# Linear-memory attention and two expert layers on one core: the second softmax computed for both halves of the heads at once, and a diagonal by ScalarE

## The chip, the core and the metric

The kernel runs on one core of a Trainium2 chip. Its engines are TensorE (PE in the profile; its weight loads are PEld), VectorE (DVE), ScalarE (ACT), GpSimd (POOL) and SyncE (SP, which here only issues DMAs). The metric is the time of one execution on the device in microseconds (us); lower is better.

## What is computed

Three layers, each fed by the one before. The attention has 4 batches of 8 heads, 576 positions, head size 64, and 32 memory slots: a first softmax over the positions turns `phi` into weights that gather keys and values into the memories, a second softmax over the 32 slots weights the values' memories. A gated layer follows, then a layer of 8 experts, each token going to one of them.

```python
def _attn_ref(q, k, v, phi):                      # 4 x 8 x 576 x 64; phi 4 x 8 x 576 x 32
    a = np.exp(phi - np.max(phi, axis=2, keepdims=True))
    a = a / (np.sum(a, axis=2, keepdims=True) + 1e-09)
    k_m = np.einsum('bhsm,bhsd->bhmd', a, k)
    v_m = np.einsum('bhsm,bhsd->bhmd', a, v)
    scores = 1.0 / np.sqrt(q.shape[-1]) * np.matmul(q, k_m.transpose(0, 1, 3, 2))
    attn = np.exp(scores - np.max(scores, axis=-1, keepdims=True))
    attn = attn / (np.sum(attn, axis=-1, keepdims=True) + 1e-09)
    return np.matmul(attn, v_m)

def _moe_ref(x, w_gate, w_val, w_out):            # x 2304 x 512, inner size 1536
    g = x @ w_gate
    return g * (1.0 / (1.0 + np.exp(-g))) * (x @ w_val) @ w_out
...
def _moe2_ref(x, w_gate, w1, w2, capacity):       # 8 experts, inner size 1024
    expert_idx = np.argmax(x @ w_gate, axis=1)
...
        out[i] = gate_w[i] * (np.maximum(x[i] @ w1[e], 0.0) @ w2[e])
```

All large matmuls are done in three passes over a high and a low part of each operand (`PASSES`), so every operand is split first: the high part by ScalarE (L115), the low part by VectorE or GpSimd (L119).

## The kernel before

The program is written as Python generators that emit instructions; a scheduler then decides the order of the instructions on each engine, and at run time each engine works through its own queue in that order. So the order in which a change's operations are emitted, and how long the scheduler takes them to be, can move other instructions too.

`attention(b)` (L254) emits one batch. The 8 heads are two halves `Q` of four, and the 576 positions two blocks `n` of `NB` = 288 columns.

- `peak(Q)` (L273) takes the maxima of `phi`: `mx` by VectorE over the positions in a partition, a transpose on TensorE into `pmx`, `top` by VectorE. To spread the 128 maxima over all partitions it makes the diagonal matrix `dg` = identity times `top` (L282, VectorE, 128x128) and multiplies it by ones on TensorE (L283). For b >= 1 ScalarE copies the result to `mg` (L285).
- `powers(Q)` (L287) subtracts (GpSimd for b >= 1, VectorE for b = 0) and takes the exponential, `ex`. `memories(Q)` (L320) multiplies `ex` by the raw keys and values `kvraw`; `normal(Q)` scales by the reciprocal sums into `kvs`; `turned(Q)` transposes into `tk` (keys) and `tv` (values).
- `queries(Q, n)` (L392) transposes q into `qt`; `products(Q, n)` (L407) multiplies: `psc`, 128 partitions (4 heads x 32 slots) x 288 columns.
- `softmax_1(Q, n)` and `softmax_2(Q, n)` (L422, L435) are the second softmax for one half and one block. VectorE turns blocks of 32x32 so that the slots lie along the free axis (`sA`, L429), takes the maxima of the 9 groups (L431), subtracts them (L432); ScalarE takes the exponential (L433); VectorE sums (L441), adds 1e-9 and inverts the 9 sums (L442, L443), multiplies (L444) and turns back into `af` (L445). For the first two batches `af` is split at once into `at`.

Eight instructions on VectorE and one on ScalarE, 16 times. `af`/`at` is the moving operand of the gated layer: `moe_in` (L632) multiplies it by `mh` (the gate's and the value's weights with the values' memories multiplied in, `mem_in` L591) into `pg` and `pv` (L644), and makes `gh` of them (`sg`: ScalarE L652, VectorE L653 and L654). `moe_out` (L658) multiplies `gh` by `wo`.

`moe_pair` (L1049) does two batches together, the inner size in 3 groups of 4 tiles of 128 columns. Batch 0's attention stands at the start, alone. Batch 1's is emitted in steps between the gate steps of batch 0 (the first half of group 0), batches 2 and 3 between the steps of the groups that follow, one step (one `yield`) per gate step. Between them all stand the weights' loads and splits: `split64` (L128) rebuilds a weight tile from its raw words by ScalarE (`mag`, L136), three VectorE instructions (L137, L139, L140) and a split, ScalarE and GpSimd.

Buffers that matter: `ph` and `kvraw` of batches 1 to 3 share two buffers (`traw`), so the next batch's `ph` waits until the memories of the batch before are multiplied; `sA`, `gh`, `qt`, `af` and others share nine (`t46`); `psc`, `pm`, `pq`, `pt`, `pmx` share four PSUM banks (`aux`).

Of the kernel before, what the change touches and what calls it, by code (L numbers as in the profile page):

```python
# [8 lines left out]
F32 = mybir.dt.float32  # L9
# [3 lines left out]
AF = mybir.ActivationFunctionType  # L13
# [8 lines left out]
def attention_moe_moe_kernel(  # L22
# [16 lines left out]
    nc = tc.nc  # L39
# [214 lines left out]
    def attention(b):  # L254
# [18 lines left out]
        def peak(Q):  # L273
# [7 lines left out]
            dg = sb.tile([128, 128], F32, tag="dg", name="dg", bufs=2)  # L281
            nc.vector.tensor_scalar(dg, ident, top, None, ALU.mult)  # L282
            nc.tensor.matmul(pm[:, 128:256], ones, dg, start=True, stop=True)  # L283
# [123 lines left out]
        def products(Q, n):  # L407
            psc = pscs[Q, n] = aux("psc")
            for hp in range(2):
                nc.tensor.matmul(psc[:, :NB], tks[Q][:, hp], qts[Q, n][:, hp], start=(hp == 0), stop=(hp == 1))  # L410

        def scores(Q, n):
            products(Q, n)
            softmax(Q, n)

        def softmax(Q, n):
            softmax_1(Q, n)
            softmax_2(Q, n)

        sAs = {}  # L420

        def softmax_1(Q, n):  # L422
            ns = slice(n * NB, (n + 1) * NB)
            psc = pscs[Q, n]
            NK = NB // MM
            sA = sAs[Q, n] = t46([128, 2, NK, MM], "sA")
            s1, s2 = sA[:, 0], sA[:, 1]
            f1 = s1.rearrange("p k m -> p (k m)")
            nc.vector.transpose(f1, psc[:, :NB])  # L429
            m1 = sb.tile([128, NK], F32, tag="m1", name="m1", bufs=2)  # L430
            nc.vector.tensor_reduce(m1, s1, AX.X, ALU.max)  # L431
            nc.vector.tensor_sub(s2, s1, m1.unsqueeze(2).to_broadcast([128, NK, MM]))  # L432
            nc.scalar.activation(s1, s2, AF.Exp, scale=float(D) ** -0.5)  # L433

        def softmax_2(Q, n):  # L435
            ns = slice(n * NB, (n + 1) * NB)
            NK = NB // MM
            s1, s2 = sAs[Q, n][:, 0], sAs[Q, n][:, 1]
            f2 = s2.rearrange("p k m -> p (k m)")
            m2 = sb.tile([128, NK], F32, tag="m1", name="m2", bufs=2)  # L440
            nc.vector.tensor_reduce(m2, s1, AX.X, ALU.add)  # L441
            nc.vector.tensor_scalar(m2, m2, 1e-9, None, ALU.add)  # L442
            nc.vector.reciprocal(m2, m2)  # L443
            nc.vector.tensor_mul(s2, s1, m2.unsqueeze(2).to_broadcast([128, NK, MM]))  # L444
            nc.vector.transpose(af[:, Q, ns], f2)  # L445
            if first:
                split(af[:, Q, ns], at[:, Q, 0, ns], at[:, Q, 1, ns], pool=True)

# [4 lines left out]
        if b == 0:  # L453
# [20 lines left out]
            products(0, 0)  # L474
            softmax_1(0, 0)
            memories(1, (1,))
            advance(p1, 1)
            softmax_2(0, 0)
            normal(1)
            queries(0, 1)  # L480
            queries(1, 1)
            advance(p1, ALL)
            turned(1)
            products(1, 0)
            softmax_1(1, 0)
            preps[0] = w
            yield
            products(0, 1)
            softmax_2(1, 0)
            softmax_1(0, 1)  # L490
            products(1, 1)
            softmax_2(0, 1)
            softmax_1(1, 1)
            softmax_2(1, 1)
            return
# [17 lines left out]
        yield  # L513
        scores(0, 0)
        turned(1)
        yield
        queries(1, 0)
        load_q(1)
        yield
        scores(1, 0)  # L520
        queries(0, 1)
        yield
        scores(0, 1)
        queries(1, 1)
        yield
        scores(1, 1)
        yield
# [707 lines left out]
```

## Time and profile before

| | |
|---|---|
| median of 3 runs | 779.68 us (779.32 to 781.97) |
| the profiled execution | 775.05 us, of which span 773.20 |
| mean granted TensorE clock | 0.95 of full |
| busy: TensorE | 698.3 us (90%), 5232 matmuls |
| busy: VectorE | 516.6 us (67%), 1156 instructions |
| busy: ScalarE | 364.8 us (47%), 763 instructions |
| busy: GpSimd | 258.3 us (33%), 286 instructions |

The shares are means over stages that differ much. In forty slices of 19.3 us the page gives the busy share in tenths (9 is 90% or more):

```profile
PE   5658878996889999979999999998999999999992
DVE  4998798989895775876076387466458556555640
ACT  2454445665642663546264075345256454444540
POOL 2465184437540360445043035131252212101101
PEclk9768887999999999999999999999999999999996
```

The attention lies in the first 13 slices. PEclk is the clock that TensorE was granted.

### The profile page before, as it was taken

To read this page: it belongs to the slowest core of one execution; us is meant where nothing else is said; L and a number is where in the kernel's file an instruction comes from. 1 tells how busy PE (TensorE), PEld (TensorE's weight loads), DVE (VectorE), ACT (ScalarE), POOL (GpSimd) and SP (SyncE) were. 2 spreads that over 40 slices of the span, in tenths; PEclk is the share of its full clock that TensorE was granted. 3 is DMA by queue.
4 is the path that set the end of the run, shared out by engine and by line. 5 is a ranking of instruction groups with operands and counts; after the bars stand their busy time and mean duration, and the time that the engine had idled before them with its cause. 6 is when DMAs were issued, how large, how long until landed. Compare 5 with 4: busy or idle time off the path is not lost. (4 is left out here: it accounts for less than half of the span.)

```text
span 773.2 us, 14235 instructions
## 1 busy us (share of the span) xinstructions
PE 698.3 (90%) x5232; PEld 663.5 (86%) x5232; DVE 516.6 (67%) x1156; ACT 364.8 (47%) x763; POOL 258.3 (33%) x286
## 2 busy tenths in 40 slices
PE   5658878996889999979999999998999999999992
PEld 4547657995889999979999998988989999999981
DVE  4998798989895775876076387466458556555640
ACT  2454445665642663546264075345256454444540
POOL 2465184437540360445043035131252212101101
PEclk9768887999999999999999999999999999999996
DMA  9977959997730621797998043153298746555520
GB/s 236 260 177 248 244 195 306 306 339 293 224 152 23 250 77 32 171 122 159 317 245 268 16 149 103 50 137 82 40 320 268 245 150 221 194 160 185 170 87 27
DMA packets 90089, 140.12 MB, mean 181 GB/s; under 512 B 28639, under 2 KB 66143, under 8 KB 84640
## 3 DMA queue, kind: packets, MB, share of 16 engines
q1 hardware_dynamic: 82560, 104.25, 46.4%
q0 software_dynamic: 7456, 34.92, 15.7%
q8 instruction: 43, 0.70, 0.5%
q14 instruction: 30, 0.25, 0.1%
HBM read 103.61 MB, written 35.79 MB: 180 GB/s over the span
## 5 line engine op out<-in xcount | busy, mean ns | idle before, releaser
L665 PE MATMUL py<-gh,wo 128*128 128x288 f32 x1152 | 165.3, 299 | 2.1 <-DVE sg L653 2.1
L665 PEld LDWEIGHTS py<-gh,wo 128*128 128x128 f32 x1152 | 156.1, 188 | 4.1 <-DVE sg L653 2.6
L644 PE MATMUL pg<-at,mh 128*128 128x288 f32 x576 | 105.2, 310 | 21.2 <-DVE sg L653 16.6
L119 POOL TENSOR_TENSOR gh<-sg,gh 128x288 fp32r<-128x288 f32 x96 | 82.7, 870 | 94.4 <-ACT gh L115 91.3
L912 PE MATMUL p<-xt,w1h 128*128 128x288 f32 x768 | 111.0, 300 | 1.0 <-DVE hh L117 1.0
L938 PE MATMUL p<-hh,w2h 128*128 128x288 f32 x768 | 108.0, 298 | 1.3 <-ACT w2h L115 1.0
L644 PEld LDWEIGHTS pg<-at,mh 128*128 128x128 f32 x576 | 85.9, 195 | 26.8 <-DVE sg L653 19.2
L644 PE MATMUL pv<-at,mh 128*128 128x288 f32 x576 | 102.7, 305 | 3.4 <-DVE sg L654 2.7
L912 PEld LDWEIGHTS p<-xt,w1h 128*128 128x128 f32 x768 | 104.2, 190 | 1.5 <-DVE hh L117 1.2
L938 PEld LDWEIGHTS p<-hh,w2h 128*128 128x128 f32 x768 | 103.2, 188 | 2.0 <-ACT w2h L115 1.3
L644 PEld LDWEIGHTS pv<-at,mh 128*128 128x128 f32 x576 | 87.2, 196 | 5.5 <-DVE sg L654 3.8
L119 DVE TENSOR_TENSOR w2h<-w2r,w2h 128x1024 fp32r<-128x1024 f32 x36 | 42.4, 1220 | 48.1 <-ACT w2h L115 48.0
L653 DVE SCALAR_TENSOR_TENSOR sg<-sg,pg 128x288 f32<-128x288 f32 x96 | 42.5, 449 | 46.2 <-ACT sg L652 45.2
L119 DVE TENSOR_TENSOR mh<-pm,mh 64x512 fp32r<-64x512 f32 (+1 forms) x92 | 62.9, 685 | 9.3 <-ACT mh L115 7.3
L652 ACT ACTIVATE sg<-pg 128x288 f32<-128x288 f32 x96 | 38.5, 409 | 64.6 <-PE pg L644 39.7
L123 POOL DMA_INDIRECT out_dram<-ot,idx x24 | 23.7, 986 | 116.3 <-DVE ot L954 113.5
L115 ACT ACTIVATE mh<-pm 64x512 fp32r<-64x512 f32 (+1 forms) x92 | 54.1, 590 | 12.1 <-PE pm L616 4.6
L675 DVE TENSOR_TENSOR yp<-py,yp 128x288 f32<-128x288 f32 x64 | 28.9, 454 | 36.8 <-PE py L665 36.2
L115 ACT ACTIVATE gh<-sg 128x288 fp32r<-128x288 f32 x96 | 41.9, 442 | 24.3 <-DVE sg L654 16.5
L119 DVE TENSOR_TENSOR w1h<-w1r,w1h 128x1024 fp32r<-128x1024 f32 x36 | 43.0, 1221 | 12.6 <-ACT w1h L115 12.5
L123 POOL DMA_INDIRECT perm<-tokid,addr x24 | 23.9, 996 | 78.8 <-DVE addr L744 46.3
L115 ACT ACTIVATE hh<-p 128x288 fp32r<-128x288 f32 x64 | 25.7, 408 | 43.1 <-PE p L912 41.3
(206 smaller groups left out, 1067.0 us busy)
## 6 DMA issues: line engine op xcount, KB each, us to landing
w1r<-in_moe_w_dram SPq DMA_DIRECT2D x36, 512.0 KB, 5.0
w2r<-in_moe_w_dram SPq DMA_DIRECT2D x36, 512.0 KB, 4.6
wgv<-wsc POOLq DMA_DIRECT2D x14, 1024.0 KB, 9.6
wsc<-wgv SPq DMA_DIRECT2D x12, 1024.0 KB, 6.8
wo<-osc POOLq DMA_DIRECT2D x10, 1024.0 KB, 10.2
wr<-in_moe_w_gate_dram SPq DMA_DIRECT2D x12, 512.0 KB, 5.2
wr<-in_moe_w_val_dram SPq DMA_DIRECT2D x12, 512.0 KB, 6.1
wor<-in_moe_w_out_dram SPq DMA_DIRECT2D x12, 512.0 KB, 4.3
```

What stands on the lines that cost most here:

```text
L115: nc.scalar.activation(hi, src, AF.Relu if relu else AF.Copy)
L119: (nc.gpsimd if pool else nc.vector).tensor_sub(lo, src, hi.bitcast(F32))
L123: ins = nc.gpsimd.indirect_dma_start(*args, **kwargs)
L644: nc.tensor.matmul(pg[gv][:, :NB], mh[:, a, Q, gv * 128 : gv * 128 + 128], at[:, Q, c, ns], start=(Q == 0 and n3 == 0), stop=(Q == 1 and n ...
L652: nc.scalar.activation(sg, pg[0][:, :NB], AF.Tanh, scale=0.5 / 256)
L653: nc.vector.scalar_tensor_tensor(sg, sg, 1.0, pg[0][:, :NB], ALU.add, ALU.mult)
L665: nc.tensor.matmul(py[:, :NB], ws[i // 2][:, i % 2, a, d * 128 : d * 128 + 128], gh[:, c, ns], start=(i == 0 and n3 == 0), stop=(i == len( ...
L675: nc.vector.tensor_add(yp[:, d], py[:, :NB], yp[:, d])
L912: nc.tensor.matmul(p1[:, :NB], st["w1"][d][:, a, f * 128 : f * 128 + 128], st["xt"][d][:, c], start=(d == 0 and n3 == 0), stop=(d == NDT - ...
L938: nc.tensor.matmul(p2[:, :NB], w2h[f // 2][:, f % 2, a, d * 128 : d * 128 + 128], hh[f][:, c], start=(f == 0 and n3 == 0), stop=(f == NF2 ...
```

## The change

The second softmax takes both halves of the heads in one tile `sA` of [128, 2, 2, 9, 32], where one half had [128, 2, 9, 32]. The transposes stay one per half (the products lie in two PSUM banks); the maxima, the subtraction, the exponential, the sums, the add, the reciprocal and the multiply become one instruction each for 576 elements (18 groups). So a block's softmax now starts when both halves' products are there. The steps are arranged anew: a batch has nine `yield`s in place of ten, with `queries` of both halves ahead of `scores(n)`, which emits both products and the softmax. Apart from that `dg` is made by ScalarE, as a copy with the scale `top`, in place of VectorE. The work of TensorE, GpSimd and the DMAs is the same; their order changes where the scheduler moves them.

```diff
@@ -279,7 +279,7 @@
             top = sb.tile([128, 1], F32, tag="top", name="top", bufs=2)
             nc.vector.tensor_reduce(top, pm[:, :128], AX.X, ALU.max)
             dg = sb.tile([128, 128], F32, tag="dg", name="dg", bufs=2)
-            nc.vector.tensor_scalar(dg, ident, top, None, ALU.mult)
+            nc.scalar.activation(dg, ident, AF.Copy, scale=top)
             nc.tensor.matmul(pm[:, 128:256], ones, dg, start=True, stop=True)
             if b >= 1:
                 nc.scalar.copy(mg[:, hs].rearrange("p h m -> p (h m)"), pm[:, 128:256])
@@ -409,42 +409,38 @@
             for hp in range(2):
                 nc.tensor.matmul(psc[:, :NB], tks[Q][:, hp], qts[Q, n][:, hp], start=(hp == 0), stop=(hp == 1))
 
-        def scores(Q, n):
-            products(Q, n)
-            softmax(Q, n)
-
-        def softmax(Q, n):
-            softmax_1(Q, n)
-            softmax_2(Q, n)
+        def scores(n):
+            products(0, n)
+            products(1, n)
+            softmax_1(n)
+            softmax_2(n)
 
         sAs = {}
-
-        def softmax_1(Q, n):
+        NK = NB // MM
+
+        def softmax_1(n):
+            sA = sAs[n] = t46([128, 2, 2, NK, MM], "sA")
+            s1, s2 = (sA[:, i].rearrange("p q k m -> p (q k) m") for i in range(2))
+            for Q in range(2):
+                nc.vector.transpose(sA[:, 0, Q].rearrange("p k m -> p (k m)"), pscs[Q, n][:, :NB])
+            m1 = sb.tile([128, 2 * NK], F32, tag="m1", name="m1", bufs=2)
+            nc.vector.tensor_reduce(m1, s1, AX.X, ALU.max)
+            nc.vector.tensor_sub(s2, s1, m1.unsqueeze(2).to_broadcast([128, 2 * NK, MM]))
+            nc.scalar.activation(s1, s2, AF.Exp, scale=float(D) ** -0.5)
+
+        def softmax_2(n):
             ns = slice(n * NB, (n + 1) * NB)
-            psc = pscs[Q, n]
-            NK = NB // MM
-            sA = sAs[Q, n] = t46([128, 2, NK, MM], "sA")
-            s1, s2 = sA[:, 0], sA[:, 1]
-            f1 = s1.rearrange("p k m -> p (k m)")
-            nc.vector.transpose(f1, psc[:, :NB])
-            m1 = sb.tile([128, NK], F32, tag="m1", name="m1", bufs=2)
-            nc.vector.tensor_reduce(m1, s1, AX.X, ALU.max)
-            nc.vector.tensor_sub(s2, s1, m1.unsqueeze(2).to_broadcast([128, NK, MM]))
-            nc.scalar.activation(s1, s2, AF.Exp, scale=float(D) ** -0.5)
-
-        def softmax_2(Q, n):
-            ns = slice(n * NB, (n + 1) * NB)
-            NK = NB // MM
-            s1, s2 = sAs[Q, n][:, 0], sAs[Q, n][:, 1]
-            f2 = s2.rearrange("p k m -> p (k m)")
-            m2 = sb.tile([128, NK], F32, tag="m1", name="m2", bufs=2)
+            sA = sAs[n]
+            s1, s2 = (sA[:, i].rearrange("p q k m -> p (q k) m") for i in range(2))
+            m2 = sb.tile([128, 2 * NK], F32, tag="m1", name="m2", bufs=2)
             nc.vector.tensor_reduce(m2, s1, AX.X, ALU.add)
             nc.vector.tensor_scalar(m2, m2, 1e-9, None, ALU.add)
             nc.vector.reciprocal(m2, m2)
-            nc.vector.tensor_mul(s2, s1, m2.unsqueeze(2).to_broadcast([128, NK, MM]))
-            nc.vector.transpose(af[:, Q, ns], f2)
-            if first:
-                split(af[:, Q, ns], at[:, Q, 0, ns], at[:, Q, 1, ns], pool=True)
+            nc.vector.tensor_mul(s2, s1, m2.unsqueeze(2).to_broadcast([128, 2 * NK, MM]))
+            for Q in range(2):
+                nc.vector.transpose(af[:, Q, ns], sA[:, 1, Q].rearrange("p k m -> p (k m)"))
+                if first:
+                    split(af[:, Q, ns], at[:, Q, 0, ns], at[:, Q, 1, ns], pool=True)
 
         if b == 0:
             tvs["alone"] = ttv()
@@ -472,26 +468,19 @@
             p0, p1 = prep_split(w, wrs, 0), prep_split(w, wrs, 1)
             advance(p0, ALL)
             products(0, 0)
-            softmax_1(0, 0)
             memories(1, (1,))
             advance(p1, 1)
-            softmax_2(0, 0)
             normal(1)
             queries(0, 1)
             queries(1, 1)
-            advance(p1, ALL)
             turned(1)
             products(1, 0)
-            softmax_1(1, 0)
+            softmax_1(0)
+            advance(p1, ALL)
             preps[0] = w
+            softmax_2(0)
             yield
-            products(0, 1)
-            softmax_2(1, 0)
-            softmax_1(0, 1)
-            products(1, 1)
-            softmax_2(0, 1)
-            softmax_1(1, 1)
-            softmax_2(1, 1)
+            scores(1)
             return
         peak(0)
         peak(1)
@@ -511,19 +500,16 @@
         normal(1)
         queries(0, 0)
         yield
-        scores(0, 0)
         turned(1)
-        yield
         queries(1, 0)
+        yield
         load_q(1)
-        yield
-        scores(1, 0)
+        scores(0)
+        yield
         queries(0, 1)
-        yield
-        scores(0, 1)
         queries(1, 1)
         yield
-        scores(1, 1)
+        scores(1)
         yield
 
     def attention_done(b):
```

The scheduler's order, up to batch 3, changes on every engine; behind that it is the same. Two places show how.

VectorE, around the first block's softmax of batch 1 (`sA` and `m` are its tiles, `mx` the maxima of batch 2's `phi`, `mh` the gate weights of batch 0's last tile, `tv` batch 1's values). Before:

```order
L429 STREAM_TRANSPOSE sA<-psc 128x288
L119 TENSOR_TENSOR mh<-pm,mh 128x512
L431 TENSOR_REDUCE m_742<-sA 128x9
L119 TENSOR_TENSOR tv<-pt,tv 128x64
L432 TENSOR_TENSOR sA<-sA,m_742 128x288
L119 TENSOR_TENSOR tv<-pt,tv 128x64
L275 TENSOR_REDUCE mx<-ph 128x128
L441 TENSOR_REDUCE m_746<-sA 128x9
L275 TENSOR_REDUCE mx<-ph 128x128
L442 TENSOR_SCALAR m_746<-m_746 128x9
```

With the change (its own line numbers: L425 to L441 are the softmax, L639 and L640 are `sg`):

```order
L275 TENSOR_REDUCE mx<-ph 128x128 x2
L640 SCALAR_TENSOR_TENSOR sg<-sg,pv 128x288
L119 TENSOR_TENSOR tv<-pt,tv 128x64
L140 SCALAR_TENSOR_TENSOR mag<-mag,wor 128x512
L119 TENSOR_TENSOR mh<-pm,mh 128x512
L639 SCALAR_TENSOR_TENSOR sg<-sg,pg 128x288
L119 TENSOR_TENSOR tv<-pt,tv 128x64
L425 STREAM_TRANSPOSE sA<-psc 128x288
L640 SCALAR_TENSOR_TENSOR sg<-sg,pv 128x288
L425 STREAM_TRANSPOSE sA<-psc 128x288
L427 TENSOR_REDUCE m_827<-sA 128x18
```

The maxima of batch 2's `phi`, which stood inside the first half's softmax, now stand ahead of two instructions of `sg`, of `mh` and of the first transpose; the two transposes stand together.

TensorE, from batch 0's third gate tile to its last (`pg`, `pv` are the gate and value matmuls, `psc` the products of batch 1). Before:

```order
L644 MATMUL pv<-at,mh 128x288 x6
L410 MATMUL psc<-qt,tk 128x288
L601 MATMUL pm<-wgv,tv 128x256 x12
L410 MATMUL psc<-qt,tk 128x288
...
L644 MATMUL pg<-at,mh 128x288 x4
L644 MATMUL pv<-at,mh 128x288 x4
L410 MATMUL psc<-qt,tk 128x288
L398 MATMUL pq<-ident,qr 128x96 x6
L410 MATMUL psc<-qt,tk 128x288 x2
```

With the change:

```order
L587 MATMUL pm<-wgv,tv 128x256 x12
L630 MATMUL pg<-at,mh 128x288 x6
L630 MATMUL pv<-at,mh 128x288 x6
L410 MATMUL psc<-qt,tk 128x288 x4
L630 MATMUL pg<-at,mh 128x288 x2
L630 MATMUL pv<-at,mh 128x288 x2
L630 MATMUL pg<-at,mh 128x288 x4
```

Each product is two matmuls. The second half's first product stood behind all matmuls of batch 0's last tile (24 of `pg` and `pv`); it now stands with the first half's, ahead of them.

## Rows read from the trace of the kernel before

**Rows 1.** Busy time by stage: stretch, length, engines, PEclk, DMA share, GB/s.

```profile
core 0: us, PE busy (x) PEld busy (x) DVE busy (x) ACT busy (x) POOL busy (x), PEclk, DMA share, GB/s
20.00:68.00 48.00, 31.12 (x177) 24.85 (x174) 45.40 (x86) 21.98 (x49) 27.38 (x28) 0.71 0.84 206
68.00:85.00 17.00, 17.00 (x147) 15.29 (x145) 13.82 (x31) 7.73 (x22) 4.79 (x6) 0.90 1.05 309
85.00:136.30 51.30, 39.36 (x268) 32.63 (x267) 44.12 (x87) 26.79 (x61) 27.32 (x26) 0.77 0.78 247
136.30:172.00 35.70, 35.70 (x267) 35.07 (x265) 32.15 (x59) 21.82 (x52) 14.42 (x14) 1.00 1.07 318
172.00:226.40 54.40, 43.53 (x346) 38.38 (x344) 51.72 (x101) 33.55 (x74) 32.77 (x32) 0.97 0.67 240
...
345.00:773.00 428.00, 405.59 (x3067) 396.89 (x3065) 238.24 (x507) 192.98 (x376) 106.09 (x116) 0.98 0.56 162
```

**Rows 2.** Waits of TensorE, 20 to 230 us: in total, times, longest.

```profile
PE pg L644 <- DVE sg L653: 14.5, 7, 4.1
```

**Rows 3.** VectorE's groups by line and form: busy us, mean ns | idle before.

```profile
L282 DVE TENSOR_SCALAR dg<-ident,top 128x128 f32<-128x128 f32 x8 | 6.0, 755 | 0.0
...
L119 DVE TENSOR_TENSOR mh<-pm,mh 64x512 fp32r<-64x512 f32 x88 | 60.2, 686 | 9.2 <-ACT mh L115 7.3
...
L432 DVE TENSOR_TENSOR sA<-sA,m 128x288 f32<-128x288 f32 x16 | 11.2, 702 | 0.2
L444 DVE TENSOR_TENSOR sA<-sA,m 128x288 f32<-128x288 f32 x16 | 10.8, 672 | 0.4
...
L441 DVE TENSOR_REDUCE m<-sA 128x9 f32<-128x288 f32 x16 | 7.1, 445 | 1.5 <-ACT sA L433 1.5
L442 DVE TENSOR_SCALAR m<-m 128x9 f32<-128x9 f32 x16 | 5.6, 349 | 0.2
...
L443 DVE RECIPROCAL m<-m 128x9 f32<-128x9 f32 x16 | 3.3, 206 | 0.3
```

**Rows 4.** Timeline of VectorE, `dg` of batches 0 and 1: start us, us.

```profile
7.98 0.29 DVE L282 TENSOR_SCALAR dg<-ident,top 128x128 f32<-128x128 f32 x1
...
47.55 1.48 DVE L282 TENSOR_SCALAR dg<-ident,top 128x128 f32<-128x128 f32 x2
```

**Rows 5.** ScalarE's groups by form, the splits of `af`.

```profile
L115 ACT ACTIVATE at<-af 128x288 fp32r<-128x288 f32 x8 | 3.5, 437 | 5.1 <-DVE af L445 5.1
...
L115 ACT ACTIVATE at<-af 128x576 fp32r<-128x576 f32 x4 | 2.5, 678 | 0.2
```

**Rows 6.** The tile `sA`: duration ns min/median/max, first and last start us.

```profile
L432 DVE TENSOR_TENSOR sA<-sA,m x16: 436/452/1545, 25.3 to 250.5; 128x288 f32<-128x288 f32 x16
```

**Rows 7.** Timeline of VectorE, batch 1, undisturbed stretch.

```profile
91.24 0.17 DVE L442 TENSOR_SCALAR m<-m 128x9 f32<-128x9 f32 x1
...
92.19 0.48 DVE L445 STREAM_TRANSPOSE af<-sA 128x288 f32<-128x288 f32 x1
92.60 0.44 DVE L429 STREAM_TRANSPOSE sA<-psc 128x288 f32<-128x288 f32 x1
```

**Rows 8.** Timeline of VectorE, batch 1's first transpose and batch 2's `mx`.

```profile
79.53 0.48 DVE L429 STREAM_TRANSPOSE sA<-psc 128x288 f32<-128x288 f32 x1 [1.48 <-PE psc L410]
...
82.29 1.36 DVE L275 TENSOR_REDUCE mx<-ph 128x128 f32<-128x640 f32 x1 [0.70 <-DMA ph<-in_phi_dram]
```

**Rows 9.** Timeline of SP's queue, the load of batch 2's `phi`.

```profile
74.88 0.33 SPq L237 DMA_DIRECT2D ph<-in_phi_dram  x1
```

**Rows 10.** Timeline of VectorE, batch 1's last `af` and the next `sg`.

```profile
111.67 0.47 DVE L445 STREAM_TRANSPOSE af<-sA 128x288 f32<-128x288 f32 x1
...
120.80 0.45 DVE L653 SCALAR_TENSOR_TENSOR sg<-sg,pg 128x288 f32<-128x288 f32 x1
```

**Rows 11.** Timeline of TensorE, the wait for that `sg`.

```profile
121.30 1.81 PE L644 MATMUL pg<-at,mh 128*128 128x288 f32 x6 [3.24 <-DVE sg L653]
```

**Rows 12.** The page's first part: busy us of each engine, share, instructions.

```profile
PE 698.3 (90%) x5232; PEld 663.5 (86%) x5232; DVE 516.6 (67%) x1156; ACT 364.8 (47%) x763; POOL 258.3 (33%) x286
```

More of the change, by code (lines that the diff above doesn't have):

```diff
@@ L513, in attention @@
         yield
-        scores(0, 0)
         turned(1)
+        queries(1, 0)
         yield
-        queries(1, 0)
         load_q(1)
+        scores(0)
         yield
-        scores(1, 0)
         queries(0, 1)
-        yield
-        scores(0, 1)
         queries(1, 1)
         yield
-        scores(1, 1)
+        scores(1)
         yield
```

## The prediction

> **What bounds the kernel now.** I read the busy times by stage first, then TensorE's waits, then the operations that the change touches. The stages [rows 1] show two kernels in a row. From 345 us to the end TensorE is busy 405.59 of 428 us at a granted clock of 0.98 (nearly its upper level, 2.4 GHz): time on VectorE is worth next to nothing there. The change ends with the last attention batch, at about 257 us, so all that it does is decided before; what it has gained by then goes to the end nearly undiminished, since TensorE works through the rest.
>
> Before 257 us the stages alternate. Call A the stretch 20 to 68 us, B 85 to 136.3, C 172 to 226.4. VectorE is busy 45.40 of 48 us in A, 44.12 of 51.3 in B and 51.72 of 54.4 in C, which is 95%, 86% and 95%; TensorE is idle 16.9 + 11.9 + 10.9 = 39.7 us of them, and its clock is low in A and B (0.71 and 0.77). In between, 136.3 to 172 us, TensorE is busy all the time: the output matmuls of the first group of gate tiles cover what VectorE does. TensorE's largest sum of waits before 230 us is for `sg` from VectorE, L653: 14.5 us in 7 waits [rows 2]. `sg` itself is short; it stands in VectorE's queue behind softmaxes and weight splits. So **time taken off VectorE's queue in A, B and C is time**, nearly one for one; elsewhere it is nothing.
>
> **The change, part by part.**
>
> *Diagonal to ScalarE.* Eight `dg` leave VectorE: 6.0 us in all, mean 755 ns [rows 3], though one alone takes 0.29 and the pair at 47.55 took 1.48 [rows 4]. The excess is waiting inside the instruction, while GpSimd works. The first two stand at 8 us, before A, where it matters little which engine does them; the other six lie in A, B and C: 6.0 - 2 x 0.29 = **5.4 us**. Lower end, if other VectorE work simply waits in their place: 6 x 0.29 = 1.7. On ScalarE the split of `af` takes 0.437 at 288 elements and 0.678 at 576 [rows 5], 0.84 ns per element; down to 128 that is 0.30 each, 1.8 us for the six, on an engine that is busy 46 to 62% in A to C. In the new order each `dg` stands right behind what its `top` waits for; behind it are the copy `mg` and the split of `af`, which VectorE delivers later anyway. Cost 0. The Trainium skill (ScalarE: Activation LUTs, What ACT_TABLE_LOAD costs) speaks against the move: a [128,1] pointer operand, as `scale=top` is, adds about 93 ns to 186 ns + 0.833 ns per element. That would be 0.39 us each, an estimate, 0.1 longer than on VectorE; no run so far has this form, but without the pointer the page gives 0.426 for 288 elements where the row has 0.437. By it the sum would be some 0.2 us worse, for the two at the start.
>
> *One set of operations for both halves.* Per block of 288 columns the two maxima, subtractions, sums, multiplies, and the small add and reciprocal, become one each; the transposes stay. A two-input operation takes 0.452 at 288 elements in the median [rows 6] and 0.686 at 512 [rows 3]: 1.045 ns per element, so 0.75 at 576, against 2 x 0.452 = 0.90. By durations that is 0.15 per pair. But in a full queue the next instruction starts some 0.07 before the one in front ends (92.19 + 0.48 against 92.60, [rows 7]), so only about 0.08 is saved. Four such pairs: 0.3 to 0.6. The 9-element add (0.17 undisturbed, [rows 7]) and the reciprocal (0.206) fold into one each: another 0.18 to 0.35. Sum 0.48 to 0.95 per block. Of eight blocks, both of the third batch and the last of the fourth lie beside TensorE's full stretches, and one straddles the end of C; for the other four it is 1.9 to 3.8, taken **2.8**.
>
> *Fewer instructions that GpSimd can hold up.* The subtraction, the multiply and the small add have means of 702, 672 and 349 ns [rows 3] against 452, 452 and 170 undisturbed: 16 x (0.25 + 0.22 + 0.18) = 10.4 us of waiting inside instructions; the longest subtraction took 1.545 [rows 6]. With half as many, half of it is the upper end, 5.2; the lower is 0, since another VectorE instruction may then meet the same GpSimd one. I take **2**, nearer the lower. The Trainium skill (SBUF — State Buffer, on the pair of ports that VectorE and GpSimd share) says that whoever comes second is blocked until the other's instruction ends, and that `tensor_reduce` never is. The sums' row agrees: mean 445, no excess. By that rule a merged operation waits once where two waited twice, and the term would be 5.2.
>
> *Moves.* Both halves' products now come before a block's softmax. For batch 1, TensorE's order pulls the second product ahead of the last 24 matmuls of batch 0's tiles, and VectorE's puts both transposes together. Before, the first half's transpose stood at 79.53 [rows 8], and its set ran while TensorE was still on those tiles; now it waits for the second product. Price: its eight operations, 2 x 0.452 + 2 x 0.445 + 0.17 + 0.206 and two transposes of 0.48, about 3.1 us, where VectorE has nothing else; 0 where its queue is full. In A it is full (95%); from 68 to 85 it is busy 13.82 of 17. I take 1. Next, the maxima over phi of batch 2 stand in the new order ahead of `sg`, of an `mh` and of the transposes. Before, their load was issued at 74.88 [rows 9] and let the first of them go at 82.29 [rows 8]. The memory matmuls of batch 1 that free its buffer move forward too, by one gate step, and the loads of k and v that they need are now ahead of a weight load in SP's queue. Price 0 if the load gains as much, 82.29 - 73.5 = 8.8 if nothing (73.5 is an estimate of when VectorE gets there: 79.53 less some 6 us of work that stood ahead and now stands behind). I take 1. In C, half a softmax of batch 2 moves out into the covered stretch and half of one of batch 3 moves in: 0. One step fewer per batch brings batch 3 forward a little; I count nothing.
>
> *Sum.* Off VectorE in A to C 5.4 + 2.8 + 2 = 10.2; times the 0.92 for which VectorE is busy there, 9.4; less 1 + 1 for the moves: **7.4 us**. What is late next there is ScalarE's weight magnitudes, then TensorE itself. The profiled execution took 775.05, so 767.6; it ran 4.6 below the median of the three runs, 779.68, and the same 7.4 off that gives **772.3 us**. The terms' bounds give from 0.92 x (1.7 + 1.9 + 0) - 3.1 - 8.8 = -8.6 (slower) to 0.92 x (5.4 + 3.8 + 5.2) = 13.2 (faster).
>
> **The rivals.** About 0.5% (3.9 us) is what a measurement here can tell from no change.
>
> *More than summed.* From 112.1, when batch 1's last `af` is done, to 120.80, `sg` stands behind weight splits [rows 10], and TensorE waits 3.24 up to 121.30 [rows 11]. If that chain simply starts earlier by the whole merged set, and C's waits close too, a third of TensorE's idle 39.7 goes: -13, 766.5. For it: few long waits, each behind work that now ends sooner. Against: the DMA engines' share was 1.07 from 136.3 to 172 [rows 1], so the next weights may not come sooner.
>
> *Little or nothing.* GpSimd's blocking falls on other instructions (`dg` 1.7, sets 1.8, no third term: 3.5 x 0.92 = 3.2) and the moves cost their 2: about 778.5. For it: the waiting comes from GpSimd's work, which is unchanged.
>
> *Slower.* The lost cover is real in all batches whose first half ran early (0, 1 and 3): 3 x 3.1 = 9.3, and the phi load adds 2, against 0.92 x (1.7 + 1.8 + 2) = 5: +6, 786. Its place is VectorE's queue ahead of the first merged transposes; it decides once VectorE sits idle there for over 2 us per batch. Against it: in A weight splits stand there.
>
> That the sets are not merged is no rival: in the built order 8 sets of 576 stand where 16 of 288 stood.
>
> **How the numbers follow.** Forecast (4 to 11 us faster) 0.50, more than summed 0.14, little 0.22, slower 0.14. So faster by over 0.5% 0.64, within it 0.22, slower 0.14. The range leaves out the end of the large gain and most of the slower case: 764 to 782. The forecast's own range is 768.5 to 776.
>
> **What would show it.** VectorE's busy time falls from 516.6 [rows 12] to 504 to 507, and none of it after 257 us; a merged operation takes 0.75 undisturbed; TensorE's wait for `sg` L653 falls from 14.5 to under 9; its output stretches begin at about 130 instead of 136.3, and 219 instead of 226.4. I am wrong if VectorE is idle for long at the merged transposes or at phi's maxima, if TensorE's idle time in C stays near 10.9, or if the gain at 257 us is not the gain at the end.

## The result, and the profile after

The changed kernel takes **770.83 us** in the median of 22 runs (765.77 to 776.75), the kernel before 778.63 in 22 runs beside it (774.18 to 788.05). The ratio is 0.9904, with a 95% interval of 0.9883 to 0.9925: 7.5 us faster (5.8 to 9.1). The forecast was 772.3 us, 7.4 faster. The profiled execution after took 770.81 us (span 769.10); that of before, 775.05, was a quick one of its kind, so the two traces differ by 4.2 us only; in the medians of all runs the two kernels are 7.8 us apart.

The page's first part (busy us, share, instructions), to [rows 12]:

```profile
PE 694.8 (90%) x5232; PEld 663.3 (86%) x5232; DVE 507.8 (66%) x1100; ACT 366.2 (48%) x763; POOL 261.9 (34%) x286
```

VectorE has lost 8.8 us and 56 instructions. The busy time by stage, to [rows 1], with the same columns:

```profile
20.00:68.00 48.00, 32.73 (x190) 26.46 (x188) 44.91 (x72) 22.75 (x50) 27.20 (x27) 0.72 0.82 211
85.00:136.30 51.30, 36.52 (x296) 32.95 (x296) 44.66 (x80) 29.21 (x68) 30.66 (x28) 0.87 0.89 287
136.30:172.00 35.70, 35.60 (x257) 34.15 (x256) 32.42 (x53) 21.38 (x47) 13.91 (x12) 1.00 0.99 317
172.00:226.40 54.40, 46.11 (x375) 41.79 (x374) 49.30 (x95) 33.14 (x74) 34.15 (x32) 0.97 0.62 218
226.40:257.00 30.60, 30.60 (x229) 30.18 (x228) 18.36 (x38) 9.86 (x22) 5.31 (x8) 1.00 0.36 135
```

VectorE is as full as before in A and B, since other work moved up; what shows is matmuls: 190, 296 and 375 in A, B and C where 177, 268 and 346 stood. (A second trace of each kernel has 191, 299 and 364 where 180, 262 and 350 stood.) TensorE's waits, 20 to 230 us, to [rows 2]:

```profile
PE pg L630 <- ACT at L115: 9.4, 2, 6.4
PE pg L630 <- DVE sg L639: 7.0, 5, 3.5
```

The wait for `sg` is halved, but a new one leads: batch 1's `at`, 6.43 us up to 107.99. In the kernel before it was:

```profile
PE pg L644 <- ACT at L115: 3.2, 2, 2.5
```

Together the two waits have fallen by 1.3 us only, from 17.7 to 16.4. VectorE's groups of the softmax and of the weight rebuild (busy us, mean ns | idle), to [rows 3]:

```profile
L140 DVE SCALAR_TENSOR_TENSOR mag<-mag,wr 128x512 int32<-128x512 int32 x24 | 23.1, 964 | 0.6
L139 DVE SCALAR_TENSOR_TENSOR wr<-wr 128x512 int32<-128x512 int32 x24 | 20.7, 863 | 0.4
L137 DVE TENSOR_SCALAR wr<-mag 128x512 int32<-128x512 int32 x24 | 16.4, 684 | 6.1 <-ACT mag L136 6.0
L139 DVE SCALAR_TENSOR_TENSOR wor<-wor 128x512 int32<-128x512 int32 x12 | 11.5, 961 | 0.1
L428 DVE TENSOR_TENSOR sA<-sA,m 128x576 f32<-128x576 f32 x8 | 9.0, 1127 | 0.1
L439 DVE TENSOR_TENSOR sA<-sA,m 128x576 f32<-128x576 f32 x8 | 7.3, 919 | 0.1
L436 DVE TENSOR_REDUCE m<-sA 128x18 f32<-128x576 f32 x8 | 6.0, 744 | 1.2 <-ACT sA L429 1.1
L437 DVE TENSOR_SCALAR m<-m 128x18 f32<-128x18 f32 x8 | 2.5, 317 | 0.1
L438 DVE RECIPROCAL m<-m 128x18 f32<-128x18 f32 x8 | 2.1, 260 | 0.1
```

and of the kernel before, the rows of the rebuild that [rows 3] did not need:

```profile
L139 DVE SCALAR_TENSOR_TENSOR wr<-wr 128x512 int32<-128x512 int32 x24 | 19.8, 824 | 0.2
L140 DVE SCALAR_TENSOR_TENSOR mag<-mag,wr 128x512 int32<-128x512 int32 x24 | 18.9, 789 | 0.6
L137 DVE TENSOR_SCALAR wr<-mag 128x512 int32<-128x512 int32 x24 | 15.1, 634 | 7.1 <-ACT mag L136 7.1
L139 DVE SCALAR_TENSOR_TENSOR wor<-wor 128x512 int32<-128x512 int32 x12 | 9.3, 779 | 0.1
```

Here is the main finding of the trace. The rebuild does the same work in both kernels, but the four rows shown have grown from 63.1 to 71.7 us. Waiting inside instructions that the softmax and `dg` no longer contain seems to have moved there; the sums below test that. Where it comes from can be seen one instruction at a time; VectorE and then GpSimd, after:

```profile
97.93 2.04 DVE L139 SCALAR_TENSOR_TENSOR wr<-wr 128x512 int32<-128x512 int32 x1
...
102.99 0.16 DVE L437 TENSOR_SCALAR m<-m 128x18 f32<-128x18 f32 x1
```

```profile
97.49 3.89 POOL L297 TENSOR_TENSOR ex<-ph,mg 128x640 f32<-128x640 f32 x2 [2.37 <-ACT mg L285]
```

A rebuild step of 0.69 us takes 2.04 while GpSimd subtracts `phi`'s maxima. Not every meeting holds VectorE up: the small add at 102.99 took its undisturbed 0.16, although GpSimd was then at a low part of `gh` (from 102.58, for 1.22 us).

On ScalarE the diagonal takes 0.394 us:

```profile
L282 ACT ACTIVATE dg<-ident,top 128x128 f32<-128x128 f32 x8 | 3.0, 394 | 2.1 <-DVE top L280 2.0
```

It has a price at the start that the row does not show. ScalarE loads its function table once, 1.28 us, ahead of its first operation. Before, that stood at 0.79 us, when nothing waited; now the first diagonal is that operation, and the load runs from 7.85 to 9.13, after the first `top` (7.50). So the first diagonal comes at 9.15 instead of 7.98, and the first memory matmul at 12.08 instead of 11.10. By batch 0's first product (21.45, before 21.85) the delay is made up.

### The profile page after: what moved, and what is told of

Read it like the earlier page. It is cut to its first block, busy times and chain, and to the rows that moved or that the text cites. A ratio compares the mean times of both kernels' runs of the same rounds, so it can differ in the third digit from the quotient of the medians.

```text
span 769.1 us, 14166 instructions
## 1 busy us (share of the span) xinstructions
PE 694.8 (90%) x5232; PEld 663.3 (86%) x5232; DVE 507.8 (66%) x1100; ACT 366.2 (48%) x763; POOL 261.9 (34%) x286
## 5 line engine op out<-in xcount | busy, mean ns | idle before, releaser
L639 DVE SCALAR_TENSOR_TENSOR sg<-sg,pg 128x288 f32<-128x288 f32 x96 | 42.2, 448 | 47.1 <-ACT sg L638 46.1
```

What stands on the lines that cost most here:

```text
L639: nc.vector.scalar_tensor_tensor(sg, sg, 1.0, pg[0][:, :NB], ALU.add, ALU.mult)
```

## Where the time came from, in the trace

Three pairs of rows give the milestones, before and then after. The first output matmuls of group 0:

```profile
136.29 2.11 PE L665 MATMUL py<-gh,wo 128*128 128x288 f32 x14
```

```profile
132.78 3.18 PE L651 MATMUL py<-gh,wo 128*128 128x288 f32 x22
```

Those of group 1:

```profile
222.11 3.36 PE L665 MATMUL py<-gh,wo 128*128 128x288 f32 x24
226.41 3.85 PE L665 MATMUL py<-gh,wo 128*128 128x288 f32 x27 [0.94 <-DVE sg L653]
```

```profile
218.73 11.44 PE L651 MATMUL py<-gh,wo 128*128 128x288 f32 x85
```

And group 2's first `sg`:

```profile
257.91 0.45 DVE L653 SCALAR_TENSOR_TENSOR sg<-sg,pg 128x288 f32<-128x288 f32 x1 [0.87 <-ACT sg L652]
```

```profile
251.22 0.46 DVE L639 SCALAR_TENSOR_TENSOR sg<-sg,pg 128x288 f32<-128x288 f32 x1 [0.84 <-ACT sg L638]
```

So A gave nothing (the second gate tile's `sg` came at 66.74 before, 66.54 after), B 3.3 and C another 3.2: 6.7 us by 257. At the last `sg` that reads `pg`, 477.10 against 473.40, 3.7 are left, and 4.1 at the end of the span.

What B gained is not a shorter wait. The stretch from the second gate tile's `sg` to the first output matmul holds 415 to 417 matmuls, the same ones in both kernels but for seven transposes. Here it is in two traces of the kernel before and then two of the kernel after (columns as in [rows 1]; the second traces come from the runs that repeat each kernel, below):

```profile
66.74:136.29 69.55, 57.11 (x416) 48.66 (x417) 59.19 (x123) 35.72 (x85) 32.59 (x32) 0.80 0.85 261
68.42:138.25 69.83, 56.30 (x417) 48.55 (x417) 59.43 (x125) 36.18 (x85) 32.84 (x32) 0.83 0.84 260
```

```profile
66.54:132.78 66.24, 49.18 (x415) 44.20 (x416) 57.39 (x109) 36.16 (x87) 35.51 (x33) 0.90 0.92 287
67.36:134.21 66.85, 50.68 (x416) 45.54 (x416) 57.50 (x109) 36.04 (x87) 35.55 (x33) 0.87 0.91 284
```

TensorE's idle time in this stretch rose from 12.4 and 13.5 us to 17.1 and 16.2. Its busy time for the same matmuls fell by some 7 us, at a granted clock of 0.90 and 0.87 where it had 0.80 and 0.83.

## The experiments

The theories. **S** (the prediction's sum): time off VectorE's queue is time, the waiting inside the diagonals included, and the moves cost 2 us. **H**: GpSimd's hold-ups are conserved; an instruction taken away brings its undisturbed price only. **O**: the new order is what pays. Six runs, with the kernel after and its repeat, part them; each cell has the ratio to the kernel before, with its 95% interval. Merged sets need both halves' products first, so the old order has none.

| | sets apart | sets merged |
|---|---|---|
| old order, `dg` on VectorE | 1.0021 (0.9997 to 1.0046) | |
| old order, `dg` on ScalarE | 1.0008 (0.9972 to 1.0043), 0.9977 (0.9945 to 1.0009) | |
| new order, `dg` on VectorE | 1.0003 (0.9974 to 1.0032) | 0.9945 (0.9918 to 0.9973) |
| new order, `dg` on ScalarE | 0.9950 (0.9920 to 0.9981) | 0.9904 (0.9883 to 0.9925), 0.9898 (0.9849 to 0.9947) |

**The kernel before again** (no edit).

> The kernel before once more, for a second trace of it and as a control of the timing: no change (ratio 1.000). The question it answers: the traced executions before and after differ by 4.1 us where the medians differ by 7.8, and of 6.7 us gained by 257 us the traced pair gives back some 3 between 257 and 345 us, where TensorE's granted clock was 0.93 in 320 to 345 us after and 1.00 before. If that give-back belongs to the change, the second trace of the kernel before has a clock of 1.00 there again, and its first gate tile of group 2 and its end stand about 6.7 and 4.1 us later than in the kernel after. If it is a matter of which execution was traced, the second trace shows a clock under 1.00 somewhere there and ends later than 773.2 us of span.

1.0021, no change as it should be. Its trace reaches group 2's first `sg` at 260.57, 2.7 later than the first trace of the same kernel, and its last `sg` at 477.46, 0.4 later. One trace of a kernel is uncertain by 2 or 3 us at a milestone, and the granted clock of 320 to 345 us is 1.00 again. The kernel after reaches them at 251.22 and 253.59 in its two traces, 473.40 and 472.83. In the mean of two, then, 6.8 us are gained by 257 us and 4.2 at 477.

**The diagonal alone.**

```diff
-            nc.vector.tensor_scalar(dg, ident, top, None, ALU.mult)
+            nc.scalar.activation(dg, ident, AF.Copy, scale=top)
```

> The kernel before, with the diagonal alone on ScalarE. By the prediction's own sum (waiting inside the eight diagonals is time of theirs and goes with them): VectorE's busy time falls by 6.0 us to about 510.6, and the time by 5.4 x 0.92 = 5.0 us (ratio 0.9936). By the rival that GpSimd's hold-ups are conserved and fall on other instructions: busy falls by 8 x 0.29 = 2.3 us only, to about 514, and the time by 6 x 0.29 x 0.92 = 1.6 us (0.998), with the weight rebuild's lines L137, L139 and L140 longer in the mean. By a second rival (the order is what counts) it is anywhere within 0.3% of no change. On ScalarE the diagonal takes 0.39 us, as in the kernel after.

> The diagonal alone on ScalarE in the order of before, once more. The runs so far: alone 1.0008 (0.9972 to 1.0043); in the new order 0.5% (with apart sets) and 0.4% (with merged sets) between the runs with and without it. If it is worth the same everywhere, about its undisturbed price of 1.6 us up to 2.5: 0.997 here. If it pays only in the new order: 1.000 again. By the prediction's sum, 5.0 us: 0.9936.

1.0008 and 0.9977, in the mean 0.6 us faster and 1.8 uncertain: S's 5.0 us is excluded, H's 1.6 is within. VectorE's busy time fell from 516.6 (517.7 in the second trace) to 515.5 and 514.7, not to S's 510.6. Most of the hold-ups turn up elsewhere: in the small add, 349 ns in the mean before, and in one row of the rebuild, 789:

```profile
L442 DVE TENSOR_SCALAR m<-m 128x9 f32<-128x9 f32 x16 | 8.2, 513 | 0.3
...
L140 DVE SCALAR_TENSOR_TENSOR mag<-mag,wr 128x512 int32<-128x512 int32 x24 | 22.4, 934 | 0.8
```

**Merged, with the diagonal back on VectorE** (the kernel after with that line undone).

> The kernel after, with the diagonal back on VectorE: merging and new order without the move to ScalarE. By the prediction's own sum: 2.8 + 2 off VectorE, times 0.92, less 2 for the moves, 2.4 us faster than before (0.997), so most of the 7.8 us is lost again. By the rival that the diagonal is worth only its undisturbed 1.6 us: 7.8 - 1.6 = 6.2 us faster than before (0.992). VectorE's busy time by the first 507.8 + 6.0 = 513.8, by the second 507.8 + 2.3 = 510.1.

0.9945: 4.3 us faster, between S's 2.4 and H's 6.2, and the interval (2.1 to 6.4) holds both. VectorE busy 510.8, near H's 510.1. The traced execution was the slowest of its twelve (779.10 us, the median is 772.58) and reaches group 2's first `sg` at 259.97, as late as the kernel before, so it shows no place for the gain.

**The new order, sets apart** (the diagonal on ScalarE).

```diff
-            m1 = sb.tile([128, 2 * NK], F32, tag="m1", name="m1", bufs=2)
-            nc.vector.tensor_reduce(m1, s1, AX.X, ALU.max)
...
+            for Q in range(2):
+                s1, s2 = sA[:, 0, Q], sA[:, 1, Q]
...
+                m1 = sb.tile([128, NK], F32, tag="m1", name="m1", bufs=2)
+                nc.vector.tensor_reduce(m1, s1, AX.X, ALU.max)
...
```

The subtraction and the exponential, and `softmax_2`, are put into a loop over the halves in the same way.

> The kernel after's order of emission (both products of a block first, nine steps), the diagonal on ScalarE, but the softmax's operations apart for each half (16 sets of 288 elements). By the prediction's sum the moves cost 2 us and the diagonal brings 5.0: about 3 us faster than before (0.996), with a longest wait of VectorE at the transposes. If merging is what pays: within 2 us of before, VectorE busy about 514 to 515. If the new order is what pays (steps that come earlier, not the cheaper set): 6 us or more faster than before (0.992 or less), with batch 1's output stretch beginning near 133 us and group 2's first gate tile near 251 us, as in the kernel after.

0.9950: 3.9 us faster (1.5 to 6.2), about S's 3; O's 6 is at the interval's end. Group 2's first `sg` comes at 253.44, as O said, but the time does not follow by as much. VectorE busy 510.6, where merging as the whole cause would have left 514 to 515.

**The new order alone** (that kernel with the diagonal on VectorE).

> The new order of emission alone: both products first and nine steps, 16 sets of 288 elements, the diagonal on VectorE as before. With the diagonal on ScalarE this order was 0.5% faster than before, and the diagonal alone on ScalarE 0.1% slower. If the order is what pays there: again about 0.5% faster (0.995). If the pair pays only together (the diagonal brings its 1.6 us where the new order puts it in a full stretch): within 0.3% of before, 0.997 to 1.003. By the prediction, which takes the moves for a cost of 2 us: 1.0026. VectorE busy 510.6 + 2.3 to 510.6 + 4 = 513 to 515.

1.0003. The order by itself brings nothing and costs nothing (2.0 us faster to 2.5 slower): VectorE busy 514.9, as expected. O falls, and so does the prediction's price for the moves as the middle value, though its 2 us is within.

Read along the table, merging brings 0.58% with the diagonal on VectorE and 0.46% with it on ScalarE, some 4 us, each 3 uncertain; the diagonal 0.53% and 0.41% in the new order, each 0.4 uncertain, and 0.07% (0.23 uncertain) in the old. One price for the diagonal everywhere, 0.24% or 1.9 us, lies within all three of these intervals. Whether it is really worth more in the new order stays open.

**Hold-ups added up.** For each kernel I took the groups of `dg`, of the subtraction, the multiply and the small add, and of the six rebuild rows, and summed count x (mean - undisturbed price). Undisturbed is 0.29 for `dg`, from the two at the start, and by medians 0.452 and 0.17 in a set apart, 0.752 (the two merged rows have 0.755 and 0.758) and 0.17 in a merged one, 0.43 (L137) and 0.69 (L139, L140) in the rebuild. In us:

| | `dg` | sets | rebuild | together |
|---|---|---|---|---|
| before, two traces | 3.7, 3.7 | 10.4, 9.8 | 17.2, 18.1 | 31.3, 31.6 |
| diagonal alone, two traces | | 10.6, 10.5 | 18.7, 18.1 | 29.3, 28.7 |
| new order alone | 2.1 | 6.9 | 22.1 | 31.1 |
| new order, diagonal on ScalarE | | 8.6 | 22.0 | 30.6 |
| merged, diagonal on VectorE | 1.6 | 4.1 | 25.6 | 31.3 |
| after, two traces | | 5.5, 5.2 | 26.2, 26.5 | 31.7, 31.7 |

The total stays at 29 to 32 us in these, whatever was merged or moved; in the five kernels further below it is 27.7 to 34.8, so the order alone moves it by some us. Over all of VectorE's groups, each priced at its median over the fourteen traces, the excess is 35.1 and 36.6 before, 35.7 and 34.4 with the diagonal alone, 33.0 and 34.2 after: of the 8.6 us that `dg` and the sets no longer hold, some 2 are gone and the rest has moved. In the main H holds for VectorE's queue.

**A step ahead of phi's maxima** (one more `yield` per batch).

```diff
+        yield
         peak(0)
         peak(1)
```

> The kernel after with one more step per batch ahead of the maxima over phi, so ten steps as before, and the maxima one gate step later. By the prediction's price for the moves: the wait of VectorE for phi's load, 2.28 us at 77.5 us in the kernel after, goes, and the time falls by up to 1 to 2 us against the kernel after (0.988 to 0.989 against before). By the rival that the shorter batch (nine steps for ten) is where the new order's gain comes from, that gain is lost: 0.994 to 0.996 against before, with group 2's first gate tile some 2 to 4 us later than in the kernel after (251.22).

1.0063 (1.0033 to 1.0092): 1.6% slower than the kernel after, some 12 us, far more than either theory said. Group 1 still begins in time (169.69 against 170.10), but group 2's first `sg` comes at 263.50 against 251.22. The windows of this kernel say how:

```profile
136.30:172.00 35.70, 35.70 (x263) 34.85 (x263) 25.76 (x44) 21.07 (x48) 10.74 (x10) 1.00 1.08 316
172.00:226.40 54.40, 42.91 (x297) 36.31 (x296) 49.39 (x90) 31.04 (x69) 34.04 (x31) 0.84 0.58 203
```

In the stretch that the output matmuls cover, VectorE does 25.76 us of work where it did 32.42 in the kernel after: 6.7 us have slid into C, batch 2's second softmax among them (its first transpose at 173.78 instead of 160.58). In C TensorE ran 297 matmuls instead of 375, at a clock of 0.84. The gate steps decide which work lies beside what, and the prediction's "One step fewer per batch brings batch 3 forward a little; I count nothing" stood on an arrangement that one step can break.

**Precedence for batch 1.**

```diff
-                with tc.high_priority(offset=50 if gen_low else 0):
+                with tc.high_priority(offset=50):
```

> The kernel after with batch 1's attention given the same precedence in the scheduler as that of batches 2 and 3: its second softmax set then stands ahead of two triples of the weight rebuild on VectorE. In the kernel after, TensorE's longest wait is 6.43 us at 107.99, for the split of batch 1's af, and 7.5 us of weight rebuild stand in VectorE's queue between 96.5 and 107 us. If that wait is VectorE's queue order: it falls to 3 us or less, and the time by 1 to 3 us against the kernel after (0.987 to 0.989 against before). If the weights are what is late (ScalarE's magnitudes and the gate weights behind them), the wait at 118.15 (3.49, for sg) grows by as much, and the time stays (0.990).

0.9920 (0.9897 to 0.9944), no gain over the kernel after. A ends 2.9 us earlier (second gate tile's `sg` at 63.68 instead of 66.54), but the wait that was to shrink grew:

```profile
109.38 0.61 PE L630 MATMUL pg<-at,mh 128*128 128x288 f32 x1 [8.04 <-ACT at L115]
```

`sg` then comes at 117.57, as after (117.65): given back in B. The expected cause of that wait was wrong: from its maxima (92.54) to `af` (108.39) the set takes 15.9 us here, where it took 13.6 after (93.38 to 106.98), with three rebuild triples begun in between all the same. Which of its steps is late stays open.

> Both edits together, the step ahead of phi's maxima and the precedence for batch 1. If both help alone, the two gains add: 0.986 to 0.988 against before. If the ten steps lose what nine had gained, it stands with the run that has ten steps alone, less what the precedence brings.

Both edits together: 1.0062 (1.0037 to 1.0088), as the added step alone; the precedence brings nothing here either.

**The kernel after again, and batch 3's first set a step later.**

```diff
         load_q(1)
+        if b == 3:
+            yield
         scores(0)
```

> The kernel after once more, for a second trace and as the measure for the two beside it on one chip: 0.990 against before (0.988 to 0.993). The first trace of it lost 2.5 us at 334.08 us to a wait for sg that four traces of other kernels do not have. If that is chance of the execution, this trace has no such wait, or has it at another length.

> The kernel after with one more step in batch 3 alone, ahead of its first softmax set. In the kernel after, that set's transposes start at 212.27, in stage C, where VectorE is busy 49.30 of 54.4 us; with the step it stands behind the first output matmuls of group 1, from 226 us, where VectorE is busy 18.36 of 30.6 us and TensorE all the time. If work in C is time and work beside the output matmuls is not: C ends earlier by what TensorE is still idle late in C, 2.3 us of 18 between 208 and 226 us, so 1 to 2.3 us against the kernel after (0.987 to 0.989 against before), although the set's VectorE work is 5. If the ten steps themselves were the fault in the run with a step ahead of phi's maxima: slower than the kernel after by some us (0.995 or more).

> That edit together with the precedence for batch 1, whose run stood at 0.992 against before (0.990 to 0.994), no gain that its interval shows over the kernel after. If the step for batch 3 brings 1 to 2 us: 0.988 to 0.990 here; if the precedence matters after all, up to 0.986.

The control gives 0.9898 (0.9849 to 0.9947); the step for batch 3 0.9919 (0.9883 to 0.9955), with the precedence 0.9941 (0.9901 to 0.9981). Both stand above what was expected for them, and no version beats the kernel after. The step did what it was to do (columns as in [rows 1]):

```profile
172.00:226.40 54.40, 47.08 (x367) 43.36 (x368) 44.79 (x84) 31.80 (x70) 33.97 (x33) 0.91 0.60 212
226.40:257.00 30.60, 30.60 (x231) 30.18 (x231) 23.11 (x47) 10.51 (x22) 4.44 (x7) 1.00 0.37 138
```

4.5 us of VectorE work left C for the covered stretch. Yet from group 1's first `sg` to group 2's it took 82.0 us (168.14 to 250.10), against 81.1 and 82.1 in the two traces of the kernel after. So, as far as one trace shows, late in C VectorE's work was not the limit, although VectorE was busy 49.30 of 54.4 us there.

## Why the prediction was right, and where it was not

The number held, 7.4 forecast and 7.5 measured. Of the three places, B and C gained; A, which the sum counted alike, gave 0.2 us in the first pair of traces and 1.1 in the second. The path and the terms did not all hold.

- *The path, "time taken off VectorE's queue in A, B and C is time", from TensorE's idle 39.7 us*: **not so in B**. There the idle time rose from some 13 us to 17, while the matmuls took 7 us less, at a higher clock. Late in C, 4.5 us of VectorE's work taken out brought nothing, by one trace. The prediction priced nothing by the clock, although it noted how low it was.
- *Diagonal, 5.4 us off VectorE, 5.0 in time*: **too large**. The step that failed is that the excess "is waiting inside the instruction" and goes with it. It stayed with GpSimd's work and moved on. By undisturbed prices the term was its own lower end, 1.7, or 1.6 in time; measured 0.6 (alone, 1.8 uncertain) to 4 (new order, 3 uncertain).
- *One set for both halves, 2.8*: the price of a merged operation was right, 0.75 predicted, 0.755 and 0.758 in the median. By durations a block saves 0.15 on each two-input operation, 0.146 on each of the maxima and sums, 0.17 on the add, 0.15 on the reciprocal: 0.91, near the upper end of 0.48 to 0.95, so 3.6 for the four blocks that count. But the discount for overlapping starts was right too: busy time, in which an overlap counts once, fell with merging by 4.1 us over the eight blocks with the diagonal on VectorE (514.9 to 510.8) and by 2.4 with it on ScalarE (510.6 to 507.8 and 508.5), 0.3 to 0.5 a block. So the term is **1.2 to 3.6**, and 2.8 lies within.
- *Fewer instructions to hold up, 2*: **near zero**, by VectorE's queue; no run prices it in time by itself. The sets' own excess fell by 4.9, from 10.4 to 5.5, almost the term's upper end. But with `dg`'s 3.7 it came back as 9.0 in the rebuild. The Trainium skill (SBUF — State Buffer, on the pair of ports that VectorE and GpSimd share) says that whoever comes second is blocked until the other's instruction ends, and that `tensor_reduce` never is; the rebuild step of 2.04 us and the merged sums' mean of 744 ns, without excess, agree. The 5.2 us that I drew from it for the whole queue does not hold, since GpSimd's instruction can hold up another of VectorE's in their place.
- *ScalarE's diagonal, 0.30 each*: **0.394**. The estimate from the Trainium skill (ScalarE: Activation LUTs, What ACT_TABLE_LOAD costs), 0.39, was right, and the extrapolation of two rows without a pointer operand was not. From 20 to 230 us it costs nothing that shows: TensorE's wait for `dg` is 2.6 us, and was 2.8. The table load of 1.28 us ahead of the first diagonal was not counted; it was made up by 22 us.
- *Moves, -2*: measured 0, within 2.5. The phi maxima do wait, 2.28 us at 77.54 (0.70 before), as priced. What pays for it was not found.

With these put in, the sum is 0.92 x (1.7 + 1.2) = 2.7 to 0.92 x (1.7 + 3.6) = 4.9 us, 2.6 to 4.8 short of what was measured, and below its interval (5.8 to 9.1). So that the number came out so near was luck: a diagonal that was 3.7 us too large and a third term that was 2 too large stood beside a cost of the moves that did not come, and beside something that the sum lacked. What that is, the runs don't settle; the clock in B is the candidate, and wasn't tried by itself.

Of the signs: VectorE's busy time, 507.8, missed 504 to 507 by the hold-ups that stayed; the wait for `sg`, 7.0, is under 9; the output stretches begin at 132.78 (130 forecast) and 218.73 (219). The second agrees by chance: before, group 1's stretch had begun at 222.11, and 226.41 was its restart after a wait of 0.94 us, so it came 3.4 us earlier and not 7.4. TensorE's idle time in C is 8.3 us and not 10.9, but the second trace of the kernel before has 8.1 as well. What is late next was neither ScalarE's weight magnitudes nor TensorE, but batch 1's `at`.

And one sign of being wrong did come: the gain at 257 us, 6.7, is not that of the traces' end. In these executions "TensorE works through the rest" failed. Near 335 us TensorE waits for `sg` 2.53 and 0.99 us in the two traces of the kernel after, 1.79 in the first of before and not at all in the second. GpSimd's queue shows why, in the kernel after:

```profile
331.35 0.92 POOL L123 DMA_INDIRECT perm<-tokid,addr  x1 [4.00 <-DMA wo<-osc]
```

The third `perm` write stood 4.00 us in GpSimd's queue, with the low parts of `gh` behind it; ScalarE's next step of `sg` waited 4.54 us for those. In the second trace the write's wait was 2.44, in the first of before 3.25, in the trace with both batch 3's step and the precedence 2.38, in the other ten 0.3 to 0.8. From group 2's first `sg` to the last it takes 218.6 to 222.2 us in the four traces with that wait and 215.7 to 217.4 in the ten without, whether they came early or late. Two of those ten, with the precedence and with batch 3's step, stood at 251.17 and 250.10 and reach the last `sg` at 468.10 and 467.13: there the gain went on undiminished. So the loss belongs to an execution and befalls either kernel; whether the kernel after meets that wait more often, four traces can't tell. Further on, up to the end, executions differ by more than the change is worth: from the last `sg` to the end of the span it takes from 292.2 to 302.1 us over the traces (order alone 767.2 - 475.0, order with the diagonal on ScalarE 772.9 - 470.8), in a part whose order is the same in all. In two that took long TensorE waited 7.6 and 7.7 us for `rows` where the first trace of before has 3.35. So the medians are the measure, and a pair of traces only shows places.

## What to carry to other kernels

Waiting inside a VectorE instruction that GpSimd holds up went, in the main, with GpSimd's instruction here: price what you remove or merge at its undisturbed duration, less what it overlaps with its neighbours, and add up the excess over all of VectorE's groups before and after to see whether it went or only moved. When work is emitted in steps beside other work, find for each step which stretch it lands in; one step more cost 12 us here, more than the prediction's whole sum. Between the same two events, read TensorE's idle and busy time apart: a stretch can shorten with more idle time, at a higher clock. And test parts in the order in which they will run, since a part's worth alone and its worth in the new order need not agree.

## What the hardware showed that was not expected

TensorE's granted clock in B. Stretches of 5 us (columns as in [rows 1]), before:

```profile
85.00:90.00 5.00, 2.13 (x10) 1.51 (x10) 4.02 (x12) 1.63 (x5) 0.79 (x1) 0.85 1.25 303
90.00:95.00 5.00, 5.00 (x16) 3.61 (x16) 3.77 (x10) 2.08 (x6) 0.79 (x1) 0.50 0.89 220
...
110.00:115.00 5.00, 3.60 (x26) 2.45 (x24) 3.80 (x4) 1.52 (x3) 5.00 (x7) 0.50 0.94 284
115.00:120.00 5.00, 3.06 (x32) 1.96 (x26) 3.42 (x6) 2.42 (x5) 1.60 (x2) 0.50 0.39 83
120.00:125.00 5.00, 3.70 (x15) 3.70 (x16) 4.97 (x10) 3.58 (x8) 2.78 (x2) 0.50 1.03 400
```

and after:

```profile
85.00:90.00 5.00, 4.29 (x27) 3.52 (x26) 4.26 (x11) 3.13 (x9) 0.44 (x1) 1.00 1.00 342
90.00:95.00 5.00, 3.29 (x26) 2.99 (x25) 3.75 (x7) 4.49 (x10) 5.00 (x6) 1.00 0.91 199
95.00:100.00 5.00, 2.81 (x20) 2.20 (x18) 4.91 (x7) 3.10 (x8) 2.63 (x3) 1.00 0.81 341
...
105.00:110.00 5.00, 2.01 (x8) 2.01 (x9) 3.86 (x6) 2.62 (x5) 5.00 (x6) 0.50 0.96 315
110.00:115.00 5.00, 4.66 (x54) 3.75 (x52) 4.47 (x5) 0.89 (x2) 2.82 (x3) 0.82 0.81 288
```

Before, TensorE was busy 2.13 of 5 us from 85 on and then ran at the lower level, 1.2 GHz, from 90 to 95; 16 matmuls filled those 5 us. From 110 to 125 it was at the lower level too. After, it is busy 4.29 of the first 5 us and stays at 2.4 GHz until 100. Taking each of the ten stretches from 85 to 135 us by its mean clock, TensorE spent 23.8 us at the lower level before and 13.6 after (20.5 and 13.7 in the second traces). That a closed wait is worth more than its length where TensorE slows down behind it would fit this, but no run shows it by itself. It does not settle the gain either: by one trace each, the new order alone has 17.1 and gained nothing, merging with the diagonal on VectorE 17.0 and gained 4.3, the new order with the diagonal on ScalarE 10.3 and gained 3.9.
